# Linear attention followed by a gated feed-forward: key sketches by two column tiles, weights loaded in halves, and the load queue's issue time in the instruction plan

## The chip, the cores and the metric

The kernel runs on one core of a Trainium2 chip. The metric is the device time of one execution in microseconds (us), lower is better. Each run also gives a span (first to last instruction, 1.7 to 2.2 us under the time) and the mean clock that was granted to TensorE. Engines are called TensorE (PE; PEld is its weight loading), VectorE (DVE), ScalarE (ACT), GpSimd (POOL) and SyncE (SP, which here only issues loads and stores). A run carries a state: "slow" when it is over 1.5% above the fastest run of the same kernel in its call. Verdicts use runs of state "fast" alone.

## The reference, cut to what matters

```python
def phi(x):                                     # x: batch, head, token, 32
    a = einsum('rd,bhsd->bhsr', S1, x)          # r = 8: a "sketch"
    b = einsum('rd,bhsd->bhsr', S2, x)
    return einsum('bhsi,bhsj->bhsij', a, b).reshape(..., 64)

q_p, k_p = phi(q), phi(k)                       # 4 batches, 4 heads, 1088 tokens
kv = einsum('bhsf,bhsd->bhfd', k_p, v)
num = einsum('bhsf,bhfd->bhsd', q_p, kv)
den = einsum('bhsf,bhf->bhs', q_p, k_p.sum(tokens)) + 1e-6
x = (num / den)                                 # -> 4352 tokens x 128
out = (relu(x @ w_gate) * (x @ w_val)) @ w_out  # inner width 1536
```

Attention of one batch must be done for its keys before its queries can give x; the feed-forward part of a group of up to 512 tokens can run as soon as that group's x is there.

## The kernel before: the parts that the change touches

The kernel is written as a list of operations with estimated durations. A list scheduler, `plan()`, simulates the engines with these estimates and emits each engine's instructions in the order that it finds. On the chip every engine runs its own queue in that order, and an instruction whose operand has not come holds all behind it. The estimates are thus only hints, but the order they lead to is fixed.

```python
SEM = {"PE": 220.0, "ACT": 220.0, "DVE": 250.0, "POOL": 200.0, "DMA": 2000.0, "SP": 2000.0}
KW = {1: (-4, 8), 2: (8, 26), 3: (35, 54)}      # window of units for a batch's key work

def load(ns, eng, t, fn, *args, **kw):          # a load as the plan sees it
    o = op(eng, t, fn, *args, **kw)
    return op("DMA", ns, lambda: None, deps=(o,))

# batch b > 0: k, q and v; the "gate" is the feed-forward unit that must have begun
k_in = (load(1650, "ACT", 200, load_k, b, at=13500.0, gate=[0, -1, 4, 20][b]),)
q_in = (load(1800, "ACT", 200, load_rest_q, b, gate=[0, 0, 10, 24][b]),)
v_in = (load(1650, "POOL", 900, load_main, nc.gpsimd, v_sb[b], v, b, gate=[0, 0, 10, 20][b], ...),)
kvr = load(600, "SP", 3000, load_rest_kv, gate=0)   # the last 64 tokens of k and v: 8 small loads
```

`load_k` first writes one element of the target on ScalarE from the value weights, so that k is issued only when the weights are there; the load itself is SyncE's.

```python
# key sketch: two halves (hf) of the tokens add up in one bank; sk[:, hf] is zero for the other half
def ab(self, x, pr, hf):
    ...
    nc.tensor.matmul(o, sk[:, hf].rearrange("p a b f -> p (a b f)"),     # 128 weight columns
                     self.kt[:, hf * GC:(hf + 1) * GC, 2 * pr:2 * pr + 2]...,   # 256 columns
                     start=(hf == 0), stop=(hf == 1), skip_group_check=True)
```

`t1` is VectorE's transpose of k that feeds it (two a batch), `t2` the transpose back. One feed-forward unit is a gate matmul, a ReLU on ScalarE, a value matmul, a product on VectorE and four output matmuls; there are 102.

## Time and profile before

| | before |
|---|---|
| time, first three runs | 124.61, 125.73, 127.17 us (median 125.73) |
| the profiled execution: time, span | 118.52 us, 116.8 us |
| TensorE, VectorE busy in it | 109.1 us (93%), 96.2 us (82%) |

### The profile page before, as it was taken

Reading aid. Unit: us, or ns where it says so; the run is one execution under the profiler, and the core shown is the slowest. Engines: PE = TensorE matmul, PEld = TensorE weight load, DVE = VectorE, ACT = ScalarE, POOL = GpSimd, SP = SyncE. Lnnn points to the kernel's source line nnn. Section 1 sums busy time; section 2 is a strip of 40 time slices with the busy share of each in tenths; the row PEclk is TensorE's granted clock in tenths of the full one; section 3 lists DMA queues with packets and bytes.
Section 4 is the critical chain, followed back from the end, with each engine's and each line's share of the span. In section 5 each row is a group of like instructions: output and inputs, shape, how many; then the busy total and the mean of one; then the engine's idle time right before and its main releaser. Section 6 shows DMA issues by size and latency. Waiting matters only on the chain.

```text
span 116.8 us, 2899 instructions
## 1 busy us (share of the span) xinstructions
PE 109.1 (93%) x1081; PEld 77.3 (66%) x1081; DVE 96.2 (82%) x204; ACT 83.2 (71%) x174; POOL 48.1 (41%) x67
## 2 busy tenths in 40 slices
PE   6999899996999999999999999999999999999920
PEld 6978768884775678456676767565675666668810
DVE  5577989968789994799997977799988799999920
ACT  5253459771445687999988876597999899998810
POOL 6868613910998995185300930171651000000000
PEclk9999999999999999999999999999999999999995
DMA  1999499679110049630001200110021002021022
GB/s 16 327 186 199 53 172 369 110 206 273 43 45 0 8 103 165 122 142 27 0 0 13 82 0 3 19 71 6 0 38 55 6 8 63 18 31 65 4 59 72
DMA packets 10945, 9.28 MB, mean 79 GB/s; under 512 B 4660, under 2 KB 9268, under 8 KB 10932
## 3 DMA queue, kind: packets, MB, share of 16 engines
q1 hardware_dynamic: 6396, 6.82, 20.4%
q0 software_dynamic: 4224, 2.25, 14.4%
q8 instruction: 8, 0.13, 0.5%
q10 hardware_dynamic: 312, 0.04, 0.2%
q14 instruction: 5, 0.04, 0.1%
HBM read 9.12 MB, written 2.23 MB: 97 GB/s over the span
## 4 chain that ended last, share of the span: by engine, by line
PE 56%; DMA 20%; DVE 15%; issue 2%; SPq 1%; DVEq 1%; ACT 1%; POOL 1%
DVE ht L574 14%; PE bank L569 12%; PE bank L584 12%; PE bank L557 12%; DMA wv<-in_moe_w_val_dram 7%; DMA q_sb<-in_q_dram 6%; DMA k_sb<-in_k_dram 6%; PE bank L409 5%; PE bank L272 3%; PE bank L446 3%; PE bank L464 2%; PE bank L337 2%; PE bank L317 1%; PE bank L371 1%; PE bank L347 1%
## 5 line engine op out<-in xcount | busy, mean ns | idle before, releaser
L574 DVE TENSOR_TENSOR ht<-g_sb,bank 128x512 f16<-128x512 f16 x102 | 65.9, 674 | 5.1 <-PE bank L569 3.3
L563 ACT ACTIVATE g_sb<-bank 128x512 f16<-128x512 f32 x102 | 59.0, 602 | 14.4 <-PE bank L557 12.0
L584 PEld LDWEIGHTS <-ht 128*128 128x128 f16 x408 | 30.7, 98 | 18.2 <-issue 1.2
L584 PE MATMUL bank<-wo,ht 128*128 128x128 f16 x408 | 38.7, 219 | 0.4 <-DVE ht L574 0.4
L569 PE MATMUL bank<-xT,wv 128*128 128x512 f16 (+1 forms) x120 | 38.8, 348 | 0.0
L557 PE MATMUL bank<-xT,wg 128*128 128x512 f16 (+1 forms) x120 | 38.2, 347 | 0.2 <-DVE xT L534 0.2
L213 POOL TENSOR_TENSOR kp<-abk 128x512 f16<-128x512 f32 x12 | 12.5, 1063 | 13.4 <-DVE abk L283 13.4
L213 POOL TENSOR_TENSOR qp<-an,abq 128x1024 f16<-128x1024 f32 (+1 forms) x9 | 15.8, 1754 | 4.1 <-DVE an L434 3.6
L569 PEld LDWEIGHTS <-wv 128*128 128x128 f16 x120 | 11.5, 100 | 3.7 <-issue 2.8
L557 PEld LDWEIGHTS <-wg 128*128 128x128 f16 x120 | 11.8, 100 | 2.2 <-issue 1.3
L272 PE MATMUL bank<-kt,sk 128*128 128x256 f32 x32 | 9.7, 394 | 1.1 <-DVE kt L261 1.1
L453 ACT COPY pt<-bank 128x512 f16<-128x512 f16 x17 | 10.0, 593 | 0.6 <-PE bank L446 0.4
L409 PE MATMUL bank<-qt,wst 128*128 128x512 f32 (+2 forms) x24 | 9.0, 477 | 0.0
L417 DVE STREAM_TRANSPOSE abq<-bank 128x512 f32<-128x512 f32 (+1 forms) x10 | 6.3, 627 | 3.3 <-PE bank L409 2.8
L421 POOL TENSOR_TENSOR bw<-abq 128x128 f32<-128x128 f32 (+1 forms) x8 | 3.5, 437 | 11.6 <-DVE abq L417 11.6
L261 DVE STREAM_TRANSPOSE kt<-k_sb 128x512 f32<-128x512 f32 x8 | 5.5, 692 | 3.1 <-DMA k_sb<-in_k_dram 3.1
L592 ACT ACTIVATE o_sb<-bank 128x512 f32<-128x512 f32 (+1 forms) x10 | 5.4, 536 | 2.9 <-PE bank L584 2.9
L470 ACT CAST xT<-bank 128x512 f16<-128x512 f32 (+1 forms) x9 | 4.9, 546 | 3.4 <-PE bank L464 3.4
L272 PEld LDWEIGHTS bank<-kt,sk 128*128 128x128 f32 x32 | 5.4, 190 | 2.2 <-ACT pt L453 1.3
L161 PE MATMUL bank<-zero 128*128 128x128 f16 x62 | 5.7, 266 | 1.1 <-DVE maskw L141 1.1
L434 POOL TENSOR_TENSOR an<-abq,rd 128x128 f32<-128x128 f32 (+1 forms) x8 | 3.1, 393 | 8.3 <-DVE rd L429 7.1
L161 PEld LDWEIGHTS <-zero 128*128 128x128 f16 x62 | 5.1, 126 | 1.2 <-DVE maskw L141 1.1
(99 smaller groups left out, 99.8 us busy)
## 6 DMA issues: line engine op xcount, KB each, us to landing
out_dram<-o_sb SPq DMA_DIRECT2D x7, 256.0 KB
q_sb<-in_q_dram SPq DMA_DIRECT2D x3, 544.0 KB, 7.2
k_sb<-in_k_dram SPq DMA_DIRECT2D x3, 512.0 KB, 6.4
v_sb<-in_v_dram POOLq DMA_DIRECT2D x4, 256.0 KB, 5.8
k_sb<-in_k_dram SPq DMA_DIRECT2D x2, 256.0 KB
q_sb<-in_q_dram SPq DMA_DIRECT2D x1, 416.0 KB
wg<-in_moe_w_gate_dram POOLq DMA_DIRECT2D x1, 384.0 KB, 6.6
wv<-in_moe_w_val_dram POOLq DMA_DIRECT2D x1, 384.0 KB, 8.0
```

Of the source, the lines that this page charges most:

```text
L161: nc.tensor.matmul(w_ps[:, 0:128], zero, zero, start=True, stop=True)
L213: eng.tensor_tensor(out=dst.rearrange("s x (i j) -> s x i j", i=R), in0=a_src[:, :, :, None].to_broadcast([dst.shape[0], n, R, R]), in1=ab ...
L261: nc.vector.transpose(self.kt[:, :, 2 * pr:2 * pr + 2], k_sb[self.b][:, 2 * pr:2 * pr + 2].rearrange("p h (c d) -> p c h d", d=D))
L272: nc.tensor.matmul(o, sk[:, hf].rearrange("p a b f -> p (a b f)"), self.kt[:, hf * GC:(hf + 1) * GC, 2 * pr:2 * pr + 2].rearrange("p c h t ...
L409: nc.tensor.matmul(self.ps[:, i * w:(i + 1) * w], wst[:, b].rearrange("p h f -> p (h f)"), self.qt.rearrange("p x t -> p (x t)")[:, i * w: ...
L417: nc.vector.transpose(self.absb.rearrange("p x f -> p (x f)"), self.ps[:, 0:n * 128])
L453: nc.scalar.copy(out=self.pt[:, lo:hi], in_=self.ps[:, lo:hi])
L557: nc.tensor.matmul(g_ps[:, y * W:(y + 1) * W], wg[:, j], xT[:, self.col:self.col + W], start=True, stop=True)
L563: nc.scalar.activation(out=self.g_sb, in_=self.g_ps, func=ACTF.Relu)
L569: nc.tensor.matmul(self.v_ps[:, y * W:(y + 1) * W], wv[:, j], xT[:, self.col:self.col + W], start=True, stop=True)
L574: nc.vector.tensor_tensor(out=self.ht, in0=self.g_sb, in1=self.v_ps, op=ALU.mult)
L584: nc.tensor.matmul(o[:, s], self.ht[:, y * W + x * 128:y * W + (x + 1) * 128], wo[:, j], start=(j == 0 and s == 0), stop=(j == NJ - 1), sk ...
```

## The change

Its intent has four parts. The key sketches of batches 1 to 3 use two column tiles of TensorE at once, 64 weight columns each, in place of matmuls padded with zeros; for this k needs another order of tokens than v, and its load falls into eight pieces. The gate and value weights come in halves. The first query group is simplified. And the plan counts the time that SyncE takes to issue loads; windows and gates were set anew. The full difference also sets other windows for query work, other priorities and three gate buffers in place of four (`"g"` in `BUFS`).

```diff
+    def load_moved(dst, src, b):
+        x = src[b, :, 0:SM, :].rearrange("h (u w t y c) d -> u w y t h (c d)", u=2, w=2, y=2, c=GC)
+        for u in range(2):
+            for w in range(2):
+                for y in range(2):
+                    n = 32 * (2 * w + y)
+                    nc.sync.dma_start(
+                        out=dst[n:n + 32].rearrange("t h (u x) -> t h u x", u=2)[:, :, u],
+                        in_=x[u, w, y])
...
-    nc.gpsimd.dma_start(out=wg, in_=moe_w_gate.rearrange("m (j f) -> m j f", j=NJ))
-    nc.gpsimd.dma_start(out=wv, in_=moe_w_val.rearrange("m (j f) -> m j f", j=NJ))
+    for js in (slice(0, NJ // 2), slice(NJ // 2, NJ)):
+        for t, w in ((wg, moe_w_gate), (wv, moe_w_val)):
+            nc.gpsimd.dma_start(out=t[:, js], in_=w.rearrange("m (j f) -> m j f", j=NJ)[:, js])
...
+        def ab(self, x, pr, n):
+            ps = self.ps[pr] = bank(x)
+            for u in range(2):
+                kt = self.kt[:, u * GC:(u + 1) * GC, 2 * pr:2 * (pr + n)].rearrange("p c h t -> p c (h t)")
+                if self.b == 0:
+                    o, w = ps, sk0[:, u].rearrange("p w y f -> p (w y f)")
+                else:
+                    o, w = ps[64 * u:64 * u + 64], sk.rearrange("p w f -> p (w f)")
+                nc.tensor.matmul(
+                    o[:, 0:n * GC * 64].rearrange("p (c x) -> p c x", c=GC), w, kt,
+                    start=self.b > 0 or u == 0, stop=self.b > 0 or u == 1)
...
-    SEM = {..., "DMA": 2000.0, "SP": 2000.0}
+    SEM = {..., "DMA": 2000.0, "SP": 100.0}
...
-    KW = {1: (-4, 8), 2: (8, 26), 3: (35, 54)}
+    KW = {1: (-19, 8), 2: (-2, 14), 3: (24, 51)}
+    LG = {1: (-1, 0, 0), 2: (6, 9, 10), 3: (17, 18, 18)}
...
-    def load(ns, eng, t, fn, *args, **kw):
+    def load(ns, issue, eng, t, fn, *args, **kw):
         o = op(eng, t, fn, *args, **kw)
+        if eng != "SP" and issue:
+            o = op("SP", issue, lambda: None, deps=(o,))
         return op("DMA", ns, lambda: None, deps=(o,))
...
+            k_in = (load(1800, 3700, "ACT", 200, load_k, b, at=13500.0, gate=LG[b][0]),)
...
-            kvr = load(600, "SP", 3000, load_rest_kv, gate=0)
+            kvr = load(600, 0, "SP", 5300, load_rest_kv, gate=0, deps=q_in[0].deps)
```

In the first query group the sketch is one matmul in place of two, and its phi goes to GpSimd alone in place of half to VectorE with a copy by ScalarE.

## The prediction

> **What bounds the kernel now.** I read the page's table of busy time first, then the chain that ended last, then busy time by window, and only then the timelines of single engines in the stretches that the windows singled out.
>
> Page, busy time by engine (busy us, share of the span, instructions):
>
> ```profile
> PE 109.1 (93%) x1081; PEld 77.3 (66%) x1081; DVE 96.2 (82%) x204; ACT 83.2 (71%) x174; POOL 48.1 (41%) x67
> ```
>
> TensorE is the candidate, but the ends of its matmuls are modelled, so 93% alone proves nothing. The windows show where it is really packed (window, length, then busy us and count for PE, PEld, DVE, ACT, POOL, then clock, DMA share, GB/s):
>
> ```profile
> 14.60:30.00 15.40, 14.19 (x137) 11.15 (x137) 13.44 (x28) 9.24 (x21) 5.54 (x6) 1.00 0.99 220
> 30.00:93.00 63.00, 63.00 (x634) 41.87 (x635) 54.13 (x105) 51.29 (x104) 31.65 (x35) 1.00 0.18 42
> 93.00:110.70 17.70, 17.70 (x178) 12.59 (x176) 17.55 (x28) 16.31 (x30) 0.00 (x0) 1.00 0.12 31
> ```
>
> I checked the middle window without the modelled ends, by slots (distance from one start to the next on the chain of waits): 65 gate and 63 value matmuls at 0.216, 248 output matmuls at 0.0555, 12 sketch pieces (L272) at 0.216, and the query, z, kv, transpose and numerator matmuls by their own slots. The sum is 62.8 of 63.0 us. So from 30 to 93 us TensorE has no hidden gap, and a slot removed there is time removed, as long as VectorE (54.1 of 63) follows. From 93 to 110.7 us TensorE and VectorE are both full: one feed-forward unit needs 2 x 0.216 + 4 x 0.0555 = 0.654 us of TensorE and one product every 0.655 us of VectorE. Nothing in the change touches that rate. In the first window the same count gives 13.3 of 15.4 us, so some 2.1 us are lost there. One loss is plain in VectorE's timeline:
>
> ```profile
> 23.31 1.84 DVE L574 TENSOR_TENSOR ht<-g_sb,bank 128x512 f16<-128x512 f16 x3
> 26.75 0.71 DVE L261 STREAM_TRANSPOSE kt<-k_sb 128x512 f32<-128x512 f32 x1 [1.59 <-DMA k_sb<-in_k_dram]
> ```
>
> and TensorE's next sketch waits 1.14 us for this transpose at 27.61. The load it waits for is batch 2's k. SyncE's queue shows why it is late (start, us):
>
> ```profile
> 13.85 0.38 SPq L88 DMA_DIRECT2D k_sb<-in_k_dram  x1
> 14.35 0.96 SPq L91 DMA_DIRECT2D q_sb<-in_q_dram  x1
> 15.35 2.71 SPq L97 DMA_DIRECT2D kr<-in_k_dram  x4
> 18.10 4.44 SPq L97 DMA_DIRECT2D vr<-in_v_dram  x4
> 22.64 0.56 SPq L88 DMA_DIRECT2D k_sb<-in_k_dram  x1
> ```
>
> The eight small remainder loads hold the queue for 7.2 us, which the kernel's plan did not know of (3.0 us), so the orders of VectorE and TensorE were fixed for a k that came earlier.
>
> Before 14.6 us the path is the first query group. The end of VectorE's part of it:
>
> ```profile
> 12.53 0.29 DVE L524 TENSOR_REDUCE dn<-prt 128x8 f32<-128x136 f32 x1
> 12.85 0.49 DVE L366 TENSOR_SCALAR kv<-bank 64x64 f16<-64x64 f32 x2
> 13.37 0.20 DVE L529 RECIPROCAL rd<-dn 128x8 f32<-128x8 f32 x1
> 13.61 0.45 DVE L531 STREAM_TRANSPOSE rd<-rd 128x256 f32<-128x256 f32 x1
> 14.16 0.42 DVE L534 TENSOR_TENSOR xT<-bank,rd 128x256 f16<-128x256 f32 x1
> ```
>
> The first gate matmul follows at 14.64. The value weights landed at about 13.6 (ScalarE's cast that reads them begins at 13.64), so they have only 1 us to spare: anything that brings xT forward by more than that runs into whole-weight loads.
>
> **What the Trainium skill says.** "TensorEngine Tiling (Array Packing)", Key Properties: tiles work independently, and changing the tiling mode drains the engine. The trace agrees with both: the eight 32-column numerator matmuls of 256 columns take a slot of 0.33 us against 8 x 0.107 = 0.86 in a row, and 0.33 is 0.12 above the ideal quarter, which I take as the drain. "TensorE: Matmul & The Clock Gate", Part 3, The mechanism: matmuls are "pc-monotone in start AND end", strict FIFO. The trace cannot say how that bears on FP32 in column tiles, since each FP32 matmul stands in it as two instructions (32 records for 16 calls at L272) and all column tiles of before are FP16. "DMA: Bandwidth & Descriptors", Rules for kernel authors: transfers to disjoint partition halves do not gain, since all use the same 16 engines. I expect that of the eightfold k load. The same page, Specifications, wants at least 512 B for line rate; the new k pieces are exactly 4 x 32 x 4 = 512 B, against 1,024 now, so bandwidth should not fall much; no run shows it yet.
>
> **The change part by part.**
>
> Sketches of batches 1 to 3. Now: four FP32 matmuls of 256 columns, each padded with zero weights for the other half, each 2 x 0.216 = 0.43 us, so 1.72 us a batch (the chain shows 0.43 for each pair of L272). After: two matmuls of 512 columns and 64 weight columns, on two column tiles. One alone costs 2 x 0.43 = 0.86, as the 512-column query sketch (L409, 0.86 to 0.91). If both tiles run fully side by side: 0.86 + 0.11 drain = 0.97, saving 0.75. But the call order is u0-first, u0-second, u1-first, u1-second; if a piece cannot start before its predecessor in the queue, u0-second waits for u0-first on the same tile, and only u0-second and u1-first overlap: 3 x 0.43 + 0.11 = 1.40, saving 0.32. If FP32 pieces do not overlap at all: 1.83, a loss of 0.1. For three batches: 2.2, 1.0 or -0.3 us. With chances 0.35, 0.5 and 0.15: 1.2 us. All of it lies in the packed stretch, so it counts in full. VectorE's transposes keep number and size.
>
> First query group. Its sketch goes from two matmuls (four records at L480, 7.77 to 8.8) to one: 0.43 us less in front of the z sums, which begin at 8.63. phi goes whole to GpSimd (0.63 there for half, so some 1.15 for all), which frees VectorE of 0.41 (L505) and ScalarE of the 0.21 copy; one of two kv copies leaves VectorE (0.25). VectorE's path to xT loses 0.41 + 0.25 = 0.66, plus part of the 0.43. Against that GpSimd carries 0.5 more, and issues four weight loads in place of two (0.55 each now, so at most 1 us), before its first k product at 7.09. GpSimd's part then ends near 11.5 and the numerator can come at about 13.0, just before the reciprocal. Net: xT 0.6 to 1.2 us earlier, say 0.9.
>
> Weights in halves. Same bytes, same queue. The first halves should land by some 10 to 12 us, the last at about 13.6 as now. By itself it gains nothing, since nothing waits for weights now; it makes the 0.9 usable, as the first three gate and value units need first halves only.
>
> k loads. 8 issues in place of 1. Two k issues took 0.92, so some 0.45 each: 3.6 us of SyncE a batch against 0.4. Batch 1's last piece leaves at about 17.4 and lands near 20, as now (transpose at 20.36). Then q, the remainders (7.2) and batch 2's k end at about 29, landing near 31 against 26.7 now. That would be worse by 4 us if VectorE's order still expected it at 26; but the new plan counts 3.7 + 0.4 + 5.3 + 3.7 us of issue, plus landing, and so puts that transpose at about 31 (0.4 of error, from 7.2 against 5.3 less its margin). Feed-forward work of batch 0 (24 units of 0.654 = 15.7 us) plus batch 1's attention covers TensorE to about 31. I expect half to two thirds of the 1.14 us stall to go: 0.6.
>
> VectorE's fills: two more small ones (0.2 to 0.3 each), one put at 16 us where VectorE has room; -0.1 together with other order effects.
>
> Sum: 1.2 + 0.9 + 0.6 - 0.1 = 2.6 us of span, and somewhat more from the re-tuned windows of work, which I can only guess at (0.4). Together 3.0. The times are some 9 us over the profiled span (125.73 against 116.8), a constant that the change does not touch: 125.7 - 3.0 = 122.7.
>
> **Rivals.**
>
> A. FP32 in column tiles does not overlap, or the drain eats it. For: nothing in the trace shows FP32 tiles overlapping, and the FIFO rule. Against: the FP16 ones do. Then only start and stall remain: 124.4.
>
> B. SyncE's queue becomes the bound. 3 x 3.2 us more issue, and remainder loads already taking 1.1 us each while other transfers are in flight. For: the wait at 26.75 is of this kind. Against: the plan now counts it. If batch 2's k slips 2 to 3 us behind its place, VectorE and TensorE stall by as much, and the gain is used up: 125 to 126.
>
> C. VectorE takes over. In the middle it has 8.9 us free of 63; TensorE giving up 2.2 leaves it at 89%. Local bunching could keep back 0.5: 123.2.
>
> D. All goes well: full overlap (2.2), 1.2 at the start, the whole 1.1 stall, tuned windows: 120.5 to 121.
>
> **Range and chances.** The middle is 122.7, D below and B above give the ends, widened by the spread of before (124.61 to 127.17 in three runs): 119.9 to 125.3. The line for "faster" is 0.98 x 125.73 = 123.2, only 0.5 us above the middle, so the chance of faster is little above a half: 0.57. Slower needs 128.2, which needs B and another stall: 0.04. The rest is 0.39.
>
> **What would show it.** The sketch of batches 1 to 3 in TensorE's timeline: about 0.97 a batch is full overlap, 1.40 half, 1.8 none. First gate matmul at about 13.7 in place of 14.64. VectorE's wait for k between 20 and 33 us under 0.6. Windows from 30 us on still full for TensorE, the tail's pitch still 0.655. The prediction is wrong if a wait on k or on the weights' second halves over 1.5 us appears, if TensorE shows gaps after 35 us, or if the first xT does not move.

## More of the kernel before

The profile cuts the span into 40 slices; a digit is the busy share of a slice in tenths. TensorE of the kernel before, and the clock granted to it:

```profile
PE   6999899996999999999999999999999999999920
PEclk9999999999999999999999999999999999999995
```

TensorE has one visible dip, in the tenth slice (26.3 to 29.2 us), and its clock never drops before the end.

## The result and the profile after

| | before | changed |
|---|---|---|
| times | 123.55, 124.61, 125.73, 127.17 us | 116.50, 116.61, 117.03, 118.92 us |
| median | 125.17 us | 116.82 us |
| profiled execution: time, span | 118.52, 116.8 us | 116.61, 114.7 us |
| TensorE, VectorE busy | 109.1, 96.2 us | 106.5, 96.0 us |

The ratio is 0.9406 (95% interval 0.9298 to 0.9515): faster by 6%. Ratios are the mean time of one kernel's fast runs over that of the other's of the same rounds, so not quite the ratio of the medians quoted. The predicted 122.7 us (119.9 to 125.3) is missed by 6 us, on the good side.

The two profiles do not show this: their spans differ by 2.1 us, and their times by 1.9. The gain of 8.4 us in the medians cannot be read from them at all. First, what they do show. The windows of the changed kernel that answer to those of before (window, length, busy us and count for PE, PEld, DVE, ACT, POOL, clock, DMA share, GB/s):

```profile
14.60:30.00 15.40, 13.92 (x145) 10.07 (x142) 13.85 (x29) 11.39 (x24) 9.56 (x10) 1.00 0.94 171
30.00:93.00 63.00, 63.00 (x635) 40.39 (x635) 55.81 (x107) 50.92 (x105) 27.65 (x31) 1.00 0.22 55
93.00:108.20 15.20, 15.20 (x154) 10.91 (x152) 15.01 (x24) 13.81 (x25) 0.00 (x0) 1.00 0.13 35
```

From 30 us on TensorE is full as before, and the end comes earlier. SyncE's queue in the stretch that was shown of before (start, us):

```profile
13.32 3.94 SPq L98 DMA_DIRECT2D k_sb<-in_k_dram  x8
18.02 0.35 SPq L103 DMA_DIRECT2D q_sb<-in_q_dram  x1
19.30 2.72 SPq L109 DMA_DIRECT2D kr<-in_k_dram  x4
22.05 2.79 SPq L109 DMA_DIRECT2D vr<-in_v_dram  x4
24.94 4.96 SPq L98 DMA_DIRECT2D k_sb<-in_k_dram  x8
```

Each k load now holds SyncE for 4 to 5 us in place of 0.4 to 0.6, and batch 2's last piece is issued only at 29.9 us, against 23.2 before. Yet VectorE does not wait for it; its transposes of batch 1's and batch 2's k:

```profile
21.66 1.30 DVE L284 STREAM_TRANSPOSE kt<-k_sb 128x512 f32<-128x512 f32 x2 [1.00 <-DMA q_sb<-in_q_dram]
...
31.59 0.71 DVE L284 STREAM_TRANSPOSE kt<-k_sb 128x512 f32<-128x512 f32 x1 [0.18 <-DMA out_dram<-o_sb]
```

(The releaser in brackets is inferred from the last semaphore event; these transposes read k, whatever the label says.) Batch 2's first transpose stands behind 13 feed-forward products in VectorE's order, where before it stood behind 9. Batch 1's k, on the other hand, is late by 1 us. TensorE's first sketch of batch 1 shows both that and what the tiles do:

```profile
23.02 1.08 PE L299 MATMUL bank<-kt,sk 128*64 128x512 f32 x4 [0.61 <-DVE kt L284]
24.03 0.40 PE L488 MATMUL bank<-pt,kv 128*32 128x256 f16 x8
```

The four pieces of a batch, each of which would hold the engine for 0.43 us alone, take a slot of 1.01 us in place of 1.72. Last, the end of the first query group on VectorE:

```profile
12.77 0.20 DVE L542 RECIPROCAL rd<-dn 128x8 f32<-128x8 f32 x1
13.00 0.45 DVE L544 STREAM_TRANSPOSE rd<-rd 128x256 f32<-128x256 f32 x1
13.48 0.19 DVE L400 TENSOR_TENSOR wst<-bank,maskw 128x32 f32<-128x32 f32 x1
13.61 0.42 DVE L547 TENSOR_TENSOR xT<-bank,rd 128x256 f16<-128x256 f32 x1
```

x is there at 14.03 us in place of 14.58. The gate matmul starts at 14.26 in place of 14.64, since a query sketch of 0.53 us was ordered in front of it.

### The profile page after: what moved, and what is told of

Its sections match the earlier page's. It is cut to its first block, busy times and chain, and to the rows that moved or that the text cites. A ratio compares the mean times of both kernels' runs of the same rounds, so it can differ in the third digit from the quotient of the medians.

```text
span 114.7 us, 2914 instructions
## 1 busy us (share of the span) xinstructions
PE 106.5 (93%) x1072; PEld 73.6 (64%) x1072; DVE 96.0 (84%) x204; ACT 82.2 (72%) x174; POOL 49.6 (43%) x69
## 4 chain that ended last, share of the span: by engine, by line
PE 71%; DMA 8%; DVE 8%; SPq 4%; ACT 2%; issue 2%; DVEq 1%; ACTq 0%
PE bank L597 16%; PE bank L570 15%; PE bank L582 15%; DVE ht L587 7%; PE bank L433 5%; DMA k_sb<-in_k_dram 5%; SPq L109 4%; PE bank L176 4%; PE bank L299 3%; DMA vr<-in_v_dram 3%; PE bank L470 3%; PE bank L361 2%; PE bank L488 2%; PE bank L341 2%; PE bank L395 1%
## 5 line engine op out<-in xcount | busy, mean ns | idle before, releaser
L576 ACT ACTIVATE g_sb<-bank 128x512 f16<-128x512 f32 x102 | 59.0, 602 | 13.7 <-PE bank L570 10.1
L597 PEld LDWEIGHTS <-ht 128*128 128x128 f16 x408 | 30.2, 99 | 16.8 <-issue 1.9
L299 PE MATMUL bank<-kt,sk 128*64 128x512 f32 (+1 forms) x20 | 5.2, 525 | 0.6 <-DVE kt L284 0.6
L423 DVE STREAM_TRANSPOSE qt<-q_sb 128x512 f32<-128x512 f32 (+1 forms) x9 | 5.7, 630 | 0.0
L361 PEld LDWEIGHTS bank<-abk 128*128 128x128 f32 x32 | 4.9, 191 | 1.0 <-issue 0.2
```

The source lines that it names most:

```text
L299: nc.tensor.matmul(o[:, 0:n * GC * 64].rearrange("p (c x) -> p c x", c=GC), w, kt, start=self.b > 0 or u == 0, stop=self.b > 0 or u == 1)
L361: nc.tensor.matmul(self.zps.rearrange("f h a j -> f (h a) j"), self.absb[:, c].rearrange("s h f -> s (h f)"), self.absb[:, c].rearrange("s ...
L576: nc.scalar.activation(out=self.g_sb, in_=self.g_ps, func=ACTF.Relu)
L597: nc.tensor.matmul(o[:, s], self.ht[:, y * W + x * 128:y * W + (x + 1) * 128], wo[:, j], start=(j == 0 and s == 0), stop=(j == NJ - 1), sk ...
```

## The experiments

Twelve runs were made, in four calls on four chips; all were correct. Each call has its own runs of the kernel before.

### The kernel before again, and what its ordinary executions look like

No edit.

> The kernel before, unchanged. The timed runs gave 123.6 to 127.2 us while its only profile shows an execution of 118.5 us, so the profile on record seems to be an unusually quick execution. Theory Q (SyncE's queue): in an ordinary execution the eight remainder loads hold SyncE longer, batch 2's k lands at 31 us or later in place of 26.7, and VectorE waits 5 us or more for it before 35 us; spans of 121 to 125 at a clock near 0.98. Theory W (whole weights): the value weights land at 18 us or later in place of 13.6, and everything after them is shifted. Theory C (clock): the granted clock of the ordinary executions is 0.95 or less and no wait grows. Theory O: the times outside the profiler carry a constant of 7 us that the change removes, and every profiled span is 116 to 117.

Measured: 122.39 us median of 6 (120.47 to 125.52), beside 123.16 of 11 for the other runs of the same kernel; ratio 1.0037 (0.9862 to 1.0211), as it must be. Time and span differ by 1.7 us in every run, so theory O, a constant outside the profiler, is out. This time the profile fell on an execution of 123.26 us. TensorE and its clock by slices:

```profile
PE   6999999960899999999999999999999999999920
...
PEclk9999999999679999999999999999999999999997
```

The first line stands for the same kernel as in "before", but the tenth slice and the next are nearly empty, and the clock falls after them. VectorE's and TensorE's lines around it:

```profile
29.89 0.71 DVE L261 STREAM_TRANSPOSE kt<-k_sb 128x512 f32<-128x512 f32 x1 [4.85 <-DMA k_sb<-in_k_dram]
```

```profile
30.75 0.67 PE L272 MATMUL bank<-kt,sk 128*128 128x256 f32 x2 [4.40 <-DVE kt L261]
```

```profile
26.00:30.00 4.00, 0.35 (x6) 0.17 (x3) 0.11 (x1) 0.59 (x2) 0.00 (x0) 1.00 1.05 297
30.00:34.00 4.00, 3.25 (x20) 2.53 (x20) 4.00 (x8) 0.00 (x0) 1.78 (x2) 0.68 0.08 30
34.00:38.00 4.00, 4.00 (x33) 2.76 (x26) 1.36 (x4) 2.06 (x4) 3.38 (x4) 0.90 0.00 0
```

Batch 2's k was issued at 23.14 us, half a microsecond later than in the quick execution, but landed at 29.9 in place of 26.75. VectorE waited 4.85 us, TensorE 4.40 in place of 1.14, and afterwards TensorE ran at half clock for some 3 us (0.68 and 0.90 in the two windows). The products tell what this costs: the first nine start within 0.15 us of those in the quick execution, the 13th starts at 36.55 us against 31.84, 4.7 us later, and the last is still 4.7 us later. Of these, 3.3 are longer waiting (4.40 against 1.14 on TensorE). The rest, 1.4, is put down to the clock: an estimate from windows of 1 us (0.71, 0.50, 0.50 and 0.59 from 31 to 35 us) gives 3.4 us at half clock, which can lose up to 1.7. Theory Q named the place and the size of the wait, though k landed at 29.9 and not at 31. Theory W is out, since ScalarE's cast that reads the value weights begins at 13.7 as before, and so is theory C, which wanted no wait to grow.

How common is it? 46 executions of the kernel before have a recorded clock. 31 of them have a mean clock under 0.985 and take 121.68 to 126.60 us (median 124.13); the other 15 have 0.986 or more and take 118.47 to 121.25. Every traced execution with the long wait is of the first kind (0.955 to 0.980, over four kernels) and every traced one without it of the second; for the untraced runs the wait is inferred from the clock. So, by their clocks, two thirds of the executions have the long wait, and the one that was profiled at first is among the quickest of all. Runs labelled fast show it too: 121.72 and 122.13 us at clocks 0.975 and 0.976 in this very run.

### The weights

```diff
-    for js in (slice(0, NJ // 2), slice(NJ // 2, NJ)):       # changed kernel
-        for t, w in ((wg, moe_w_gate), (wv, moe_w_val)):
-            nc.gpsimd.dma_start(out=t[:, js], in_=w...[:, js])
+    nc.gpsimd.dma_start(out=wg, in_=...)
+    nc.gpsimd.dma_start(out=wv, in_=...)
```

> The changed kernel with its gate and value weights loaded whole again, orders of all engines unchanged. If the halves are what took the 8 us, this comes back to 122 or more (ratio to before above 0.975). If they are only what lets the first units start, it loses at most 1 us: 117 to 118, ratio about 0.945. I expect the second: nothing waited for weights in the profile of before.

Measured: 118.07 us median of 4; ratio to before 0.9757 (0.9615 to 0.9898), unclear at 2%. By the ratio named beforehand (above 0.975) this would just count for the halves, but before's fast runs, 120.80 and 121.20 us, were by their clocks executions without the long wait, and the times did not come back to 122. The single times are 117.32, 117.40, 118.74 and 118.76, and the changed kernel in its runs has the same two groups (116.5 to 117.0, and 118.92). The profile fell on a run of the upper group and shows what divides them: the start.

### A slow start

No kernel of its own, but two traces of the changed kernel, the one on record and that of a repetition further down; TensorE's first key sketches (start, us):

```profile
5.41 1.95 PE L299 MATMUL bank<-kt,sk 128*128 128x256 f32 x8
```

```profile
6.24 3.71 PE L299 MATMUL bank<-kt,sk 128*128 128x256 f32 x8
```

The same eight pieces take twice as long in the second, and the first product starts at 19.76 us in place of 17.16. In the first trace TensorE's pieces reach full speed near 4.5 us, in the second only near 9.9. The end of the execution is 2.2 us later. The granted clock in the profile reads 1.00 in both (4 to 12 us), so it does not show this; "half clock" at the start is inferred from the doubled times. A variant of the kernel before has such a start in its trace too (the next run: six pieces take 2.87 us in place of 1.51), and the times of 120.3 to 121.3 us at a high clock suggest it for the kernel before. Such starts are the second reason for the spread; nothing shows that the change alters how often they come. Compared like for like, whole weights cost 0.6 us (117.36 against the 116.71 mean of the lower group), with two runs on one side and three on the other, on different chips: within the halves' worth of 1 us that was expected, and no more than that can be said.

### Halves alone, on the kernel before

```diff
-    nc.gpsimd.dma_start(out=wg, ...); nc.gpsimd.dma_start(out=wv, ...)
+    (the four half loads; the releasing casts read wv[0:1, NJ - 1, 0:1])
```

> The kernel before with only its weights loaded in halves, the casts that release k and q reading the last half. Theory W: 119 or less. Theory Q: 125 within 1 us, ratio 0.99 to 1.01.

Measured: 124.89 us median of 4, three of them 124.25 to 126.09 and one 118.73; no ratio could be formed. The profile (126.09 us) shows VectorE waiting 4.9 us for k as before. In it k of batch 1 was also issued later (15.85 us in place of 13.9), so it is not a pure test of the halves; but the long wait does not go away with them. Theory W falls.

### SyncE's time alone, in the plan of the kernel before

```diff
-    SEM = {..., "DMA": 2000.0, "SP": 2000.0}
+    SEM = {..., "DMA": 2000.0, "SP": 100.0}
+        if eng != "SP" and issue: o = op("SP", issue, ...)     # 400 for each k and q
-            kvr = load(600, "SP", 3000, load_rest_kv, gate=0)
+            kvr = load(600, 0, "SP", 5300, load_rest_kv, gate=0, deps=q_in[0].deps)
```

> The kernel before, planned with SyncE's issue time (0.4 us for each k and q load, 5.3 us for the remainder loads, 0.1 in place of 2.0 us behind SyncE); k still in one load, one sketch layout, windows as before. Theory Q: most of the 8 us comes back, 117 to 120, because VectorE and TensorE no longer queue behind a k that has not landed. Theory W or C: 124 to 126, ratio 0.99 to 1.01.

Measured: 124.02 us median of 4 (122.17 to 125.30), ratio 1.0167 (0.9857 to 1.0476): nothing came back in the median (the verdict is unclear). This was a miss for my first theory, that SyncE's queue as such is the cause. The order shows why: the plan moved batch 2's first key transpose only from behind 9 products to behind 10, and k came at 30.0 us, with a wait of 3.85. With one issue of 0.4 us per k, the plan still believes in a k long before 30.

This led to a sharper theory, again called O (for order; not the constant of the first run): what counts is how many products stand in front of batch 2's key transposes in VectorE's queue.

### One number in the plan of the kernel before

```diff
-        kv, wf, kb = add_k(b, rest if b else rest0, (4400.0, 5600.0) if b == 0 else (0.0, 0.0),
+        landed = {0: (4400.0, 5600.0), 2: (30500.0, 30500.0)}.get(b, (0.0, 0.0))
+        kv, wf, kb = add_k(b, rest if b else rest0, landed,
```

> The kernel before with one number of its plan changed: batch 2's key transposes may not be planned before 30.5 us, so they stand behind 12 feed-forward products on VectorE in place of 9. No load, no instruction and no wait is taken out. Theory O (order: VectorE and TensorE stand in their queues behind a k that in ordinary executions lands only at 30 us, and the long idle also costs TensorE's clock): the wait of VectorE for k near 30 us falls from 4.8 us to under 1, no clock below 0.95 after it, times of 117 to 119.5 against 122 to 125 of before. Theory P (the arrival itself is what counts, through the work that depends on batch 2): the wait moves elsewhere and the time stays over 122.

Measured: 118.04, 118.50, 120.69 and 120.82 us; ratio 0.9891 (0.958 to 1.0201), unclear, because the fast runs of before were quick executions.

> The kernel before with batch 2's key transposes planned for 30.5 us, a second time and with more runs, since four runs left the interval open. Theory O: no run with a mean clock under 0.985 (before: 24 of 35 runs so far), times in two groups, near 118.3 and, with a start at half clock, near 120.7; median 2 to 5 us under before of the same call. If the first four were luck: about two thirds of the runs at 122 to 126 with a clock under 0.985.

Measured: 117.63, 117.91, 117.93, 117.96, 120.02 and 120.90 us, against 118.47 to 126.04 (median 123.67) for before. The ratio of fast runs is 0.9937 (0.9904 to 0.9970), since before's two fast runs, 118.47 and 118.74, were its executions without the wait; it measures the quick case only. The distribution is the result: of ten runs of the edited kernel, none has a clock under 0.986, where two thirds of before's have. In the trace:

```profile
29.59 0.70 DVE L261 STREAM_TRANSPOSE kt<-k_sb 128x512 f32<-128x512 f32 x1
```

k is read at the same time as in the slow execution of before, and VectorE does not wait for it. Was k late in these executions at all? The trace does not date its landing, but it shows the bytes moved: from 22 to 26 us the quick execution of before moved 139 GB/s, the slow one 56, and the two traced ones of this kernel 47 and 52 (last column; before, before again, this kernel's first trace):

```profile
22.00:26.00 4.00, 4.00 (x45) 3.46 (x43) 3.16 (x6) 2.87 (x8) 1.71 (x2) 1.00 0.49 139
22.00:26.00 4.00, 4.00 (x45) 3.46 (x43) 3.04 (x6) 2.87 (x9) 1.59 (x2) 1.00 0.55 56
22.00:26.00 4.00, 4.00 (x43) 3.44 (x41) 4.00 (x8) 2.87 (x8) 1.97 (x2) 1.00 0.41 47
```

At 47 or 52 GB/s some 0.2 MB arrive in these 4 us, less than half of k's 0.5 MB. So up to 26 us the transfers ran as in the slow execution, k had not landed when VectorE would have been ready for it in the old order (25.0 us in the slow execution), and here nothing waited for it. The loads and the numbers of instructions at work on each engine are those of before (1,081 on TensorE, 204 on VectorE); only the order differs. It is not these two transposes alone, since the scheduler then orders what follows anew (batch 3's first key transpose stands behind 32 products in place of 33). Theory O holds, and P falls.

### The other way round: the changed kernel, planned without SyncE's time

```diff
-    SEM = {..., "SP": 100.0}
+    SEM = {..., "SP": 2000.0}
-        if eng != "SP" and issue: o = op("SP", issue, lambda: None, deps=(o,))
-            kvr = load(600, 0, "SP", 5300, load_rest_kv, ...)
+            kvr = load(600, 0, "SP", 3000, load_rest_kv, ...)
```

> The changed kernel, planned without SyncE's issue time (no 3.7 us per k load, 3.0 us for the remainder loads, 2.0 us behind SyncE): batch 2's first key transpose then stands behind 8 products in place of 13, while k still takes eight issues. Theory O: VectorE waits 4 us or more for batch 2's k, TensorE's clock drops after it, 121.5 to 125, as slow as before. Theory P: within 1 us of the changed kernel, 116 to 118.

Measured: 127.36 us median of 4 (125.24 to 128.16), ratio to before 1.0532 (1.0126 to 1.0938), unclear at 2% but above 1: 10 us slower than the changed kernel's median on record, and slower than before, whose fast runs in this call were by their clocks executions without the long wait. Column tiles, halves and all the rest are in it. VectorE's transpose of batch 2's k, and the windows after it:

```profile
32.41 0.71 DVE L284 STREAM_TRANSPOSE kt<-k_sb 128x512 f32<-128x512 f32 x1 [4.64 <-DMA out_dram<-o_sb]
```

```profile
34.00:38.00 4.00, 4.00 (x32) 2.88 (x31) 2.71 (x7) 1.50 (x5) 1.06 (x1) 0.50 0.08 28
38.00:42.00 4.00, 4.00 (x12) 1.50 (x13) 2.13 (x4) 0.95 (x3) 1.35 (x2) 0.50 0.01 2
```

TensorE waited 4.75 us, and its clock then stood at half for 10 us (32 to 42 us). TensorE was at work for 8.3 of these, so the clock cost about 4 us by estimate, nearly as much as the wait. Batch 1's transposes, placed earlier as well, waited another 2.2.

### Does k come late because of what shares the way with it?

```diff
-   q_in = (load(1800, "ACT", 200, load_rest_q, b, gate=[0, 0, 10, 24][b]),)     # before
+   q_in = (load(1800, "ACT", 200, load_rest_q, b, gate=[0, 0, 18, 24][b]),)
-   v_in = (... gate=[0, 0, 10, 20][b], at=13000.0),)
+   v_in = (... gate=[0, 0, 18, 20][b], at=13000.0),)
```

> The kernel before with batch 2's q and v loads released at feed-forward unit 18 in place of 10; VectorE's order around batch 2's k is the same (behind 9 products). Theory X (k shares the 16 DMA engines with 0.54 MB of q and 0.5 MB of v issued within 1 us of it): k lands near 26.5 us in every execution, the wait for it is 1 to 2 us, times 118 to 120.5. Theory Y (SyncE's queue, held by the remainder loads until 23 us, is the whole reason): k lands at 29 to 30 as before, times 122 to 125.

Measured: 120.06, 120.50, 121.58 and 126.98 us; ratio 1.0095 (0.9866 to 1.0325), unclear. The profile is of the first:

```profile
27.27 0.71 DVE L261 STREAM_TRANSPOSE kt<-k_sb 128x512 f32<-128x512 f32 x1 [1.92 <-DMA k_sb<-in_k_dram]
```

k was issued at 23.06 and read at 27.27, 4.2 us later, where the slow execution of before took 6.7. But the quick execution of before took only 4.1 (issued at 22.64, read at 26.75) with q and v issued beside it. So this one trace, of the fastest of four runs, does not separate the theories. Nor do the times: three of the four runs have a high clock (0.988 to 0.995), and if each run has one chance in three of that, three or more of four come out so by luck in 11% of cases. The fourth has a clock of 0.961, so the long wait still comes, and theory X, which asked for every execution, does not hold as stated. What delays k in the slow executions stays open.

### The sketch alone put back

```diff
-                if self.b == 0:
+                if True:                                   # zero-padded weights for all batches
                     o, w = ps, sk0...
-                    start=self.b > 0 or u == 0, stop=self.b > 0 or u == 1)
+                    start=u == 0, stop=u == 1)
-        load_moved(k_sb[b], k, b)
+        load_main(nc.sync, k_sb[b], k, b)
```

> The changed kernel with only the sketch of batches 1 to 3 put back: two 512-column matmuls of 128 weight columns (half of them zeros) for each half that add up, k in one load and one layout; the order of every engine as in the changed kernel. Theory T (column tiles are worth what their slots say, 1.01 against 1.72 us a batch): +2.1 us, 118.5 to 119.5. Theory S (the eightfold k load costs SyncE as much as the tiles save): 116 to 117.5. If the tiles were what took the 8 us: above 122.

Measured: 116.56, 116.63, 116.70 and 117.18 us; ratio to before 0.9767 (0.9591 to 0.9943). The changed kernel's lower group, on another chip, is 116.50 to 117.03. The tiles save 2.1 us of TensorE's slots and change the time by next to nothing: theory S. The product starts of the two traces show where it goes. At the 6th product the changed kernel is 1.07 us later than this one (22.89 against 21.82 us), because batch 1's k needs eight issues (TensorE's wait of 0.61 at 23.02). Batch 2's saving is used up in the same way: its first key transpose starts 0.82 us later than here (31.59 against 30.77), its sketch 0.66 us later (35.07 against 34.41). At the 25th product the two are level (48.13 against 48.22). Only batch 3's sketch starts at the same time in both (49.72), and what it saves stays: the changed kernel is 0.75 ahead at the 30th product (52.84 against 53.59) and at the last one. At the end of the span 0.3 us of it are left (114.7 against 115.0), and 0.1 in the time.

### The tiles where there is time for the load

```diff
-                if self.b == 0:
+                if self.b < 2:                             # batch 1 as batch 0: old sketch
...
-        load_moved(k_sb[b], k, b)
+        if b < 2: load_main(nc.sync, k_sb[b], k, b)        # and one load
+        else: load_moved(k_sb[b], k, b)
```

> The changed kernel with batch 1 alone put back to the old sketch and the single k load; batches 2 and 3 keep the column tiles; every engine's order as in the changed kernel. With theory S (for batch 1 the eight issues bring k about 1.1 us later, in a stretch where TensorE has to wait for it, and so use up the tiles' 0.75 us) this is the quickest: product 6 near 22.5 us as with the old sketch, the 0.75 us of batches 2 and 3 both kept, so 0.5 to 1.2 us under the changed kernel of the same call, near 115.8. If batch 2's tiles are also lost, within 0.4 us of it.

The same, planned with its own costs (0.4 us of SyncE and 1.76 us of sketch for batch 1):

> The same kernel, but planned with what batch 1 now costs (0.4 us of SyncE in place of 3.7, 1.76 us of sketch). The plan then puts batch 2's key transposes behind 9 products in place of 13, although its eight pieces cannot land much before 30 us. Theory O: VectorE waits 2 to 4 us for them and the time is 118.5 to 122, slower than the same loads in the old order. If the plan's timing is right in itself: 115.5 to 116.5.

And the changed kernel beside them on the same chip:

> The changed kernel again, to have it on the same chip as the two others: 116.5 to 117.2, with one execution in four or so near 119 (a start at half TensorE clock), ratio to before 0.94 to 0.97.

| | runs | median |
|---|---|---|
| before | 118.59 to 125.93 (11) | 123.83 |
| changed kernel | 116.22, 116.64, 116.71, 117.35; 118.78, 118.86, 119.09, 119.11 | 118.06 |
| batch 1 old, changed kernel's order | 115.46, 115.93, 116.23, 116.31; 118.49, 118.77 | 116.27 |
| batch 1 old, planned anew | 117.17, 117.47, 117.59, 117.69, 117.71; 119.57 | 117.64 |

The mean of the fast runs is 115.98 us with batch 1 old and 116.73 for the changed kernel, 0.75 apart (the slow ones, by their times, have the slow start: 118.63 and 118.96). With four fast runs on each side this is only just clear of their scatter, and under the 2% of a verdict. The traces leave it open as well: the last product starts at 108.31 us here and at 108.33 in the changed kernel on record, though the first one started 0.56 us later here. It is the best version found, but that it is quicker than the changed kernel is likely, not shown.

Planning it anew lost 1.5 us against the kept order (117.53 mean of fast runs against 115.98), though my expectation had the reason wrong. Batch 2's transposes stand behind 9 products, but its k had come by 29.0 us, with a wait of only 0.16. What waited was batch 1:

```profile
20.52 1.30 DVE L284 STREAM_TRANSPOSE kt<-k_sb 128x512 f32<-128x512 f32 x2 [0.82 <-DMA k_sb<-in_k_dram]
```

They stand behind 3 products in place of 5. TensorE's wait for them is 0.80 us, about half of the loss. Where the other half goes was not settled.

## Why the prediction was wrong

**The step that failed** is "The times are some 9 us over the profiled span (125.73 against 116.8), a constant that the change does not touch". The constant is 1.7 to 2.2 us in every run that gives both. The other 7 us were the difference between the profiled execution and the timed ones, and this was in sight: the profiled execution's own time was 118.52 us, under every timed run. Two thirds of before's executions have, by their clocks, a wait of 4 to 5 us for batch 2's k with a drop of TensorE's clock behind it, and there are starts that cost 2.2 us. The prediction took the rare case for the rule and valued the removal of the wait at 0.6 us. In the one ordinary execution of before that was traced, the wait and the clock cost 4.7 us more than in the quick one.

**The mechanism** was named, in rival B ("VectorE and TensorE stall by as much") and in the reading of VectorE's wait at 26.75, as something that might strike the changed kernel. It had been striking the kernel before all along. The plan of before put the transposes behind 9 products for a k that comes at 27 to 30 us; the changed plan puts them behind 13, for a k that comes at 31. It does so because k's eight issues are counted. The change did not bring k earlier, it brought it later, and expected it later.

**What follows for the 8.4 us.** Among executions with neither a slow start nor the long wait, before takes 118.47 to 118.74 us (four runs) and the changed kernel 116.22 to 117.35 (seven): 1.9 us between the means. That is the quantity the prediction was in fact estimating, and it said 3.0. The rest of the difference of the medians is the mix of executions: the long wait, with its clock, is gone. The order alone, put into the kernel before, brought its median from 123.67 to 117.95 us, 5.7 of the 8.4. That the result lay on the good side of the forecast was luck: an effect that the prediction had not valued outweighed what fell short.

**Point by point.**

- Sketches. "0.97 a batch is full overlap": right, 1.01, and full overlap had been given only a third of the chances. The likelier case, half overlap because of the order of the pieces, did not occur: the four pieces start in pairs, at 23.02, 23.03, 23.50 and 23.51. That the 0.15 us over the 0.86 of one tile is the drain is not shown. But the 2.1 us saved did not "count in full": 0.75 us was left in the traces, at batch 3, and next to nothing in the times, since the load that the tiles need came too late for batches 1 and 2.
- First query group. xT came 0.55 us earlier, not 0.9, and the first gate matmul 0.38. VectorE's shorter path did appear (the reciprocal at 12.77 in place of 13.37).
- Weights in halves. "By itself it gains nothing" is not refuted; some 0.6 us may hang on it, from two runs against three on different chips.
- k loads. "Batch 1's last piece ... lands near 20, as now" was wrong: the transposes start at 21.66, after a wait of 1.0. The eight issues took 3.94 us, as worked out (3.6). "Batch 2's k ... landing near 31" and "so puts that transpose at about 31" were right (31.59, wait 0.18).
- Rivals. A is refuted. B is the cause, but of the time before. C: VectorE was busy 55.8 of 63 us in the middle, and no sign of it as the bound was found.
- "A wait on k or on the weights' second halves over 1.5 us": none; the tail's pitch (from one product's start to the next) is still 0.655.

What is open: which event delays k in the slow executions, how the 1.9 us divide between the first query group, the halves and the new windows, priorities and buffers, and half of the loss of the replanned version.

## What to carry to other kernels

Compare the profiled execution's own time with the timed runs before reading anything from its trace; if it lies outside them, profile again until the trace is of an ordinary execution. Where each engine's order is fixed at build time, put a consumer behind enough other work for the latest ordinary arrival of its load, not the earliest: being placed too late cost nothing that could be seen here, being placed 3 us too early cost the wait and then TensorE's clock. A saving on the busiest engine is worth what the data it needs can keep up with, so ask for each place where it is used when its load can be there.

## What the Trainium skill lacked or had wrong

- "TensorE: Matmul & The Clock Gate", HAM oscillation — how this bites in real kernels: idle gaps over about 3.4 us bring half clock. The runs put the line lower: no drop after waits of 1.14, 1.47 and 2.16 us, but half clock after one of 3.15 us (the kernel before planned with SyncE's time), as after 4.40, 4.47 and 4.75. And the page's 3.4 us of sustained work to come back (Part 1) is too short for one of them: half clock lasted 3.4 us in the kernel before, but 10 us (32 to 42 us) in the changed kernel planned without SyncE's time, 8.3 of them with TensorE at work.
- The same page, Part 1, says that the time at which full speed comes varies by half a microsecond, by where the window lies. TensorE was at work from 1.1 us on with warm-up matmuls, and reached full speed near 4.5 us in some executions and near 9.9 in others. The cost was 2.2 us.
- No page gives a time for FP32 matmuls on column tiles, nor says how the strict order of matmuls (the same page, Part 3) bears on them; each stands as two pieces in the trace. Four such pieces on two column tiles take 1.01 us, against 0.43 for one piece alone: the tiles overlap, but for 0.15 us.
- "DMA: Bandwidth & Descriptors", Issuing engines are not separate DMA queues, calls the issue time "usually small relative to the DMA itself". That holds for one issue here (0.43 us, against a median of 3.6 from issue to landing), but not for eight in a row, which held SyncE for 3.94 us. Nor is it constant: the four small v loads of 32 KB took 4.44 to 6.22 us to issue where batch 1's k went as one load just before them, and 2.6 to 2.8 where it went as eight. Why was not settled.
